# Attention and gated FFN on one core: v kept for two chunks, one limit and one guard for two heads, no empty-row test, the weights' last bits added as integers by GpSimd

## The chip, the cores and the metric

The kernel runs on one core of a Trainium2 chip, as one program. The metric is the device time of one execution in microseconds. The five engines are called as the profile calls them: PE (matmul and transpose; PEld is its weight load), DVE (vector), ACT (scalar, activations), POOL (GpSimd) and SP, which here only issues DMAs. Each engine takes its instructions in the order in which the program lists them, and waits on semaphores for the others.

## The reference, cut to what matters

Eight batches, eight heads, 576 positions, head width 64; the FFN goes from 512 to 1024 and back. The scores are cut at the row's maximum less tau. The softmax sums over what is left, and 1e-9 guards the division.

```python
scores = scale * np.matmul(q, k.transpose(0, 1, 3, 2))
thresh = np.max(scores, axis=-1, keepdims=True) - tau
scores = np.where(scores >= thresh, scores, -1000000000.0)
attn = np.exp(scores - np.max(scores, axis=-1, keepdims=True))
attn = attn / (np.sum(attn, axis=-1, keepdims=True) + 1e-09)
x = np.matmul(attn, v)                      # then heads side by side: (B, S, 512)
...
h = np.maximum(x @ w_in, 0.0)               # (B, S, 1024)
conv_out = sum(conv_w[k] * hp[:, k:k + S, :] for k in range(3))   # hp: h padded by one
out = (h * (1.0 / (1.0 + np.exp(-conv_out)))) @ w_out
```

The weights w_in, conv_w and w_out are 64-bit floats. The kernel gets them as pairs of 32-bit words (low word first) and makes two 32-bit parts, high and low, of each.

## The kernel before, in words

**Tiles.** Heads are taken in pairs, four pairs for a batch. The 576 rows of a pair are five tiles, four of 128 rows and one of 64. The five tiles are cut into two chunks: tiles 0 and 1, and tiles 2 to 4. A *unit* is one tile of one pair (160 in all, 20 for a batch, and units 0 to 7 are batch 0's first chunk). A unit with 128 rows handles the two heads one after the other, the 64-row unit handles both at once.

**A unit** (function `unit`). PE makes the scores of a head into a PSUM buffer `ps_s` (two of them; line 573 in batch 0 and in the 64-row units, line 580 elsewhere). DVE takes the negated maximum into a small tile `few` (588), somebody takes the limit, maximum less tau (594 on DVE or POOL, 592 on ACT), ACT takes the exponential into `em` (597), and DVE masks it against the limit and sums the row (600). Then come three small steps for both heads at once: the guard, sum plus 1e-9 (617), the test for an empty row, 1/576 where the sum is 0 (621), and the reciprocal (624). POOL multiplies `em` by the reciprocal and adds the empty-row term (633, "the norm"). The normalized tile is transposed on PE through `ps_t` (692) and evacuated by ACT into `eT` (687), or, for 28 units, written to DRAM through `parts` and read back transposed by DMA. `attend` multiplies `eT` by v (747, 756).

**v.** `load_v` loads 128x576 words for each pair and chunk, into two buffers in turn, so that each pair's v is loaded twice in a batch.

**The FFN** of a chunk begins when its four pairs are done. `mm1` multiplies by w_in (784), then ACT, DVE and POOL make the gated product in high and low parts (799, 806, 813, 811, 821, 333), and `mm2` multiplies by w_out (842). It is spread between the units of the next chunk.

**The weights** (function `split`, 16 pieces of 128x512 and one of 128x24 for conv_w). A piece arrives as pairs of words in `stage` (one of four buffers) and becomes one 32-bit float `stage_f` in five steps: absolute value of the upper word (ACT, 377), clamp (POOL, 380), shift and mask (DVE, 383), sign and top bit (DVE, 386), and last the top three bits of the lower word put in with an OR (DVE, 389). A copy in reduced precision is the high part (ACT, 400), and the rest is the low part, by PE and ACT for 12 pieces (405, 406, 409) and by POOL for four (333).

**What sets the order.** A planner (`Plan.run`) writes the order of each engine's instructions before the program is built: a list of operations with an engine, an assumed duration, what they read and write, how many buffers a tag has, and a due rank. It goes through assumed time and gives each engine the most urgent operation that is ready. For some operations another engine may step in (limit, guard, norm). The chip then follows these queues in that order, whatever the real durations are. Any edit of an operation or its assumed cost therefore writes all five queues anew.

## Time and profile before

| what | value |
|---|---|
| median of 3 runs | 911.69 us (911.31 to 913.77) |
| span of the profiled execution, first to last instruction | 910.8 us |
| PE busy | 874.6 us, 96% |
| DVE busy | 751.2 us, 82% |
| ACT busy | 673.8 us, 74% |
| POOL busy | 603.5 us, 66% |
| HBM read, written | 58.88 MB, 25.95 MB |

The profile gives the span of the profiled execution; what lies around it is the difference to the time of a run, 0.9 us to the median. Busy shares are means over the whole span. The first 150 us differ from the rest: there batch 0's attention runs beside the preparation of the weights, and the FFN has only begun. The table of slices at the top of the page shows it, and the tables by stretch below are read for that reason.

### The profile page before, as it was taken

How to read it: one execution, taken by the hardware profiler on the slowest of the kernel's cores; microseconds unless marked ns; L12 is line 12 of the kernel's file. 1: busy time of each engine (PE TensorE's matmuls, PEld its weight loads, DVE VectorE, ACT ScalarE, POOL GpSimd, SP SyncE). 2: the span in 40 equal slices, each digit the busy share in tenths (PEclk: the TensorE clock that was granted, in tenths of full speed). 3: DMA queues.
4: the chain of work that ended last, by engine and by line, in shares of the span. 5: the costliest groups of instructions: out<-in, count | busy, mean ns of one | idle time of the engine just before them, and what ended most of it. 6: DMA issues, size and time to landing. Idle time of an engine off the chain costs nothing.

```text
span 910.8 us, 19147 instructions
## 1 busy us (share of the span) xinstructions
PE 874.6 (96%) x6056; PEld 708.6 (78%) x6056; DVE 751.2 (82%) x1871; ACT 673.8 (74%) x1459; POOL 603.5 (66%) x1027
## 2 busy tenths in 40 slices
PE   5978799999999999999999999999999999999998
PEld 3545577878878788888788797887888878887896
DVE  5988999988988689987889789996988779997542
ACT  4878687878777777777768687877867778776642
POOL 2656778875767677685767767776776758675322
PEclk9989899999999999999999999999999999999999
DMA  6555257667764667647665377557667276654000
GB/s 213 155 162 170 57 143 197 149 178 181 198 175 113 163 175 198 158 116 202 169 157 157 117 201 191 140 118 202 173 176 179 89 187 159 181 137 112 13 24 35
DMA packets 148260, 137.02 MB, mean 150 GB/s; under 512 B 85312, under 2 KB 116288, under 8 KB 148160
## 3 DMA queue, kind: packets, MB, share of 16 engines
q1 hardware_dynamic: 147296, 133.90, 55.3%
q10 hardware_dynamic: 864, 1.90, 0.6%
q8 instruction: 49, 0.80, 0.4%
q14 instruction: 51, 0.42, 0.2%
HBM read 58.88 MB, written 25.95 MB: 93 GB/s over the span
## 4 chain that ended last, share of the span: by engine, by line
PE 73%; ACT 8%; DVE 6%; POOL 5%; DMA 4%; issue 3%; SPq 2%; ACTq 0%; POOLq 0%; DVEq 0%
PE po L842 20%; PE ph L784 16%; PE pa L756 12%; PE ps_s L580 11%; PE ps_t L692 9%; PE ps_s L573 3%; ACT em L597 2%; POOL em L633 2%; DVE em L600 2%; ACT eT L687 2%; PE pa L747 2%; DVE few L588 2%; DMA q<-in_qd_dram 1%; SPq L513 1%; DMA q<-q 1%
## 5 line engine op out<-in xcount | busy, mean ns | idle before, releaser
L633 POOL TENSOR_SCALAR em<-em,few 128x576 f32<-128x576 f32 x287 | 262.8, 924 | 29.9 <-DVE few L624 22.1
L600 DVE SCALAR_TENSOR_TENSOR em<-ps_s,few,em 128x576 f32<-128x576 f32 x288 | 230.5, 812 | 25.4 <-ACT em L597 17.1
L588 DVE TENSOR_REDUCE few<-ps_s 128x1 f32<-128x576 f32 x288 | 211.5, 748 | 39.3 <-PE ps_s L573 22.0
L597 ACT ACTIVATE em<-ps_s,few 128x576 f32<-128x576 f32 x288 | 210.5, 741 | 35.8 <-DVE few L588 31.5
L784 PE MATMUL ph<-x,w1h 128*128 128x322 f32 (+1 forms) x1024 | 233.7, 304 | 0.6 <-ACT hp L799 0.5
L687 ACT ACTIVATE eT<-ps_t 128x512 f32<-128x512 f32 (+2 forms) x360 | 168.0, 487 | 24.5 <-PE ps_t L692 22.4
L784 PEld LDWEIGHTS ph<-x,w1h 128*128 128x128 f32 x1024 | 173.1, 189 | 4.7 <-issue 3.0
L692 PE MATMUL ps_t<-ident,em 128*128 128x128 f32 x1060 | 157.8, 280 | 6.5 <-POOL em L633 5.1
L580 PE MATMUL ps_s<-ks,q 128*128 128x288 f32 x896 | 156.8, 306 | 5.3 <-DMA q<-q 2.1
L784 PE MATMUL ph<-x,w1l 128*128 128x322 f32 (+1 forms) x512 | 151.3, 295 | 0.0
L692 PEld LDWEIGHTS ps_t<-ident,em 128*128 128x128 f32 x1060 | 126.5, 143 | 31.5 <-POOL em L633 14.9
L580 PEld LDWEIGHTS ps_s<-ks,q 128*128 128x128 f32 x896 | 129.2, 189 | 20.2 <-issue 8.2
L333 POOL TENSOR_TENSOR gl<-t,gh 128x255 fp32r<-128x255 f32 (+9 forms) x192 | 119.6, 637 | 28.5 <-ACT gh L821 27.5
L756 PE MATMUL pa<-eT,v 128*64 128x320 f32 (+1 forms) x1024 | 132.1, 410 | 0.0
L842 PE MATMUL po<-w2h,gh 128*128 128x512 f32 x288 | 117.9, 409 | 0.3 <-ACT hp L799 0.3
L756 PEld LDWEIGHTS pa<-eT,v 128*64 128x64 f32 x1024 | 70.4, 137 | 59.3 <-issue 15.8
L842 PE MATMUL po<-w2l,gh 128*128 128x512 f32 x288 | 113.3, 393 | 0.0
L842 PE MATMUL po<-w2h,gl 128*128 128x512 f32 x288 | 113.1, 393 | 0.1
L806 DVE SCALAR_TENSOR_TENSOR t<-hp,cr 128x321 f32<-128x321 f32 (+1 forms) x128 | 75.6, 594 | 28.0 <-ACT hp L799 28.0
L784 PEld LDWEIGHTS ph<-x,w1l 128*128 128x128 f32 x512 | 96.8, 189 | 0.2
L813 ACT ACTIVATE t<-t,cm 128x321 f32<-128x321 f32 (+1 forms) x128 | 68.0, 535 | 25.2 <-DVE t L806 12.2
L811 DVE SCALAR_TENSOR_TENSOR t<-t,hp 128x321 f32<-128x321 f32 (+1 forms) x128 | 73.1, 573 | 11.4 <-ACT t L813 9.8
(80 smaller groups left out, 1104.1 us busy)
## 6 DMA issues: line engine op xcount, KB each, us to landing
q<-q SPq DMA_DIRECT2D x336, 64.0 KB, 2.1
v<-in_vc_dram SPq DMA_DIRECT2D x64, 288.0 KB, 3.8
rows<-parts SPq DMA_DIRECT2D x28, 576.0 KB, 3.3
k<-in_kp_dram SPq DMA_DIRECT2D x35, 320.0 KB, 3.5
out_dram<-ot SPq DMA_DIRECT2D x36, 256.0 KB, 2.3
xk<-in_kt_dram SPq DMA_DIRECT2D x28, 288.0 KB, 3.4
ks<-xk SPq DMA_DIRECT2D x56, 144.0 KB, 3.3
xq<-in_qt_dram SPq DMA_DIRECT2D x56, 128.0 KB, 2.9
```

The costliest lines, as they stand in the source:

```text
L333: engines[e].tensor_tensor(dst, x, y, op=ALU.subtract)
L580: nc.tensor.matmul(ps[:, c, :CH], lhsT=q[:, h, o:o + n], rhs=k[:, h, c * CH:(c + 1) * CH], start=(i == 0), stop=(i == 1))
L588: nc.vector.tensor_reduce(few[:rows, nm], ps[:rows, :, :CH], op=ALU.max, axis=mybir.AxisListType.XY, negate=True)
L597: nc.scalar.activation(view(), ps[:rows, :, :CH], AF.Exp, bias=few[:rows, nm])
L600: nc.vector.scalar_tensor_tensor(view(), ps[:rows, :, :CH], few[:rows, th], view(), op0=ALU.is_ge, op1=ALU.mult, accum_out=few[:rows, total])
L633: engines[e].tensor_scalar(sl, sl, by, to, op0=ALU.mult, op1=ALU.add)
L687: "act", act(w, True), lambda dst=dst, src=src: nc.scalar.activation(dst(), src(pt), AF.Copy),
L692: nc.tensor.transpose(out=pt[:, at:at + P], in_=em[:, int(b * P):int(b * P) + P], identity=ident[:])
L756: nc.tensor.matmul(pa[j * D:(j + 1) * D, :w], lhsT=vt[:, blk, :], rhs=eT[:, :w // D, blk, :], start=False, stop=(r == 3))
L784: nc.tensor.matmul(ph[:, :an], lhsT=w1[w][:, cb, fs], rhs=xs[cb][:, h, :an], start=(cb == 0 and i == 0), stop=(cb == NCB - 1 and i == 2))
L806: nc.vector.scalar_tensor_tensor(t[:, :kn], hp[:, k:kn + k], cr[:, j, f:f + 1], y, op0=ALU.mult, op1=ALU.add)
L842: nc.tensor.matmul(po[:], lhsT=x[:, f, at:at + P], rhs=w[:, f, :], start=(f == 0 and i == 0), stop=(f == NFB - 1 and i == 2))
```

## The change: what it does

- `load_v`: the second chunk of batches 1 to 7 takes the v tile that the first chunk loaded. The tag has four buffers in place of two, and 36 loads are left of 64. `parts` has one buffer in place of two, which makes room.
- `unit`: one limit for both heads, a subtraction of two tensors (`ntau` with two columns, less the negated maxima). It reads both heads' maxima, so the first mask now comes after the second maximum.
- The guard is a sum of two tensors, the sums and a constant `least` of 576 x 2^-80. The empty-row test is gone; the norm adds 2^-80 to each weight and multiplies by the reciprocal, which gives 1/576 in an empty row. ACT can no longer take the norm.
- `split`: ACT takes the top 16 bits of the lower word, times 2^-13, as an integer (0 to 8) into the lower word's place (`rounded`), and POOL adds it to `stage_f` as a 32-bit integer (`f4`), where DVE had the OR.
- The planner's assumed DMA times are changed (`put`, `cross`).

```diff
-        op(queue, issue, fn, ring=rows * (n * 0.225 + 4) * 0.0737, **kw)
+        op(queue, issue, fn, ring=rows * n * 0.0149, **kw)
...
+        def rounded():
+            tops = flat().bitcast(U16).rearrange("p (f four) -> p f four", four=4)
+            nc.scalar.activation(words(I32)[0], tops[:, :, 1], AF.Copy, scale=2.0 ** -13)
+
         def f4():
-            nc.vector.scalar_tensor_tensor(v(U32), words()[0], 29, v(U32), op0=ALU.logical_shift_right, op1=ALU.bitwise_or)
+            nc.gpsimd.tensor_tensor(v(I32), v(I32), words(I32)[0], op=ALU.add)
...
+        op("act", act(n), rounded, w=[lo], ahead=w)
...
-        op("dve", 100 + n * 1.3, f4, w=[a], r=[lo], ahead=w, port=True)
+        op("pool", pool(n), f4, w=[a], r=[lo], ahead=w, port=True)
...
     def load_v(i, b, p):
-        vt = plan.buf(wk, "v", 2, [P, NBLK, D], F32, f"v_{i}")
+        if b and chunks[pairs[i][0]].new[0]:
+            return vts[i - NP]
+        vt = plan.buf(wk, "v", VB, [P, NBLK, D], F32, f"v_{i}")
...
-                    engines[e].tensor_scalar(few[:rows, th], few[:rows, nm], -1.0, ntau[:rows], op0=ALU.mult, op1=ALU.add)
+                    subtract(e, few[:rows, limits], ntau[:rows, :m], few[:rows, tops])
...
-            op("dve", 125, limit, w=[(few, ("th", h))], r=[(few, ("nm", h)), (ntau, 0)], ahead=a, other=[("pool", 260), ("act", 110)])
-            op("dve", 738, mask, w=[(em, h), (few, ("sum", h))], r=[(ps, 0), (few, ("th", h))], ahead=a)
+            late.append(mask)
+            if h == m - 1:
+                op(
+                    "dve", 125, limit, w=[(few, "th")], r=[(few, ("nm", x)) for x in range(m)] + [(ntau, 0), (ntau, 1)], ahead=a,
+                    other=[("pool", 260), ("act", 110)]
+                )
+        for h in range(m):
+            op("dve", 738, late[h], w=[(em, h), (few, ("sum", h))], r=[(pss[h], 0), (few, "th")], ahead=a)
...
-            engines[e].tensor_scalar(few[:rows, inverse], few[:rows, sums], 1e-9, 1.0, op0=ALU.add, op1=ALU.mult)
-
-
-        def even(e):
-            engines[e].tensor_scalar(few[:rows, shift], few[:rows, sums], 0.0, 1.0 / S, op0=ALU.is_equal, op1=ALU.mult)
-
+            engines[e].tensor_tensor(few[:rows, inverse], few[:rows, sums], least[:rows, :m], op=ALU.add)
...
-                    engines[e].tensor_scalar(sl, sl, by, to, op0=ALU.mult, op1=ALU.add)
+                engines[e].tensor_scalar(sl, sl, LEAST, few[:rows, 6 + h:7 + h], op0=ALU.add, op1=ALU.mult)
...
-        parts = plan.buf(wk, "parts", 2, [P, 2, 2 * S], U16, f"parts_{u}")
+        parts = plan.buf(wk, "parts", 1, [P, 2, 2 * S], U16, f"parts_{u}")
```

The queues are written anew. Three places show how. The first is POOL's queue while the last eight weight pieces are prepared. `stage_f` is a piece, `em` a unit's weights, `few` its small tile. Before:

```order
L594 TENSOR_SCALAR few_781<-few_781,ntau 128x1 x2
L380 TENSOR_SCALAR stage_f<-stage_f 128x512
L617 TENSOR_SCALAR few_781<-few_781 128x2
L633 TENSOR_SCALAR em_790<-em_790,few_781 128x576 x2
L380 TENSOR_SCALAR stage_f<-stage_f 128x512
L594 TENSOR_SCALAR few_849<-few_849,ntau 128x1 x2
L617 TENSOR_SCALAR few_849<-few_849 128x2
```

The same two units and their neighbours in POOL's queue now (line 399 is the integer add, 386 the clamp, 645 the norm):

```order
L399 TENSOR_TENSOR stage_f<-stage_f,stage_522 128x512
L386 TENSOR_SCALAR stage_f<-stage_f 128x512
L399 TENSOR_TENSOR stage_f<-stage_f,stage_568 128x512
L645 TENSOR_SCALAR em_735<-em_735,few_730 128x576 x2
L386 TENSOR_SCALAR stage_f<-stage_f 128x512
L638 TENSOR_TENSOR few_799<-few_799,least 128x2
L399 TENSOR_TENSOR stage_f<-stage_f,stage_649 128x512
L386 TENSOR_SCALAR stage_f<-stage_f 128x512
L645 TENSOR_SCALAR em_829<-em_829,few_799 128x576 x2
```

Where a unit's small steps stood between clamps and norms, integer adds stand now, two of them ahead of one norm.

The second place is DVE's queue at unit 80, in the middle of the program, before (588 is the maximum, 594 the limit, 600 the mask, 806 a tap of the FFN):

```order
L588 TENSOR_REDUCE few_5674<-ps_s_0_5662 128x1
L588 TENSOR_REDUCE few_5674<-ps_s_1_5669 128x1
L594 TENSOR_SCALAR few_5674<-few_5674,ntau 128x1
L600 SCALAR_TENSOR_TENSOR em_5686,few_5674<-ps_s_0_5662,few_5674,em_5686 128x576
L806 SCALAR_TENSOR_TENSOR t_0_5716<-hp_0_5290,cr 128x255
L600 SCALAR_TENSOR_TENSOR em_5686,few_5674<-ps_s_1_5669,few_5674,em_5686 128x576
```

and now (603, 339 and 615 are the maximum, the limit of both heads and the mask):

```order
L603 TENSOR_REDUCE few_5511<-ps_s_0_5497 128x1
L603 TENSOR_REDUCE few_5511<-ps_s_1_5505 128x1
L339 TENSOR_TENSOR few_5511<-ntau,few_5511 128x2
L615 SCALAR_TENSOR_TENSOR em_5525,few_5511<-ps_s_0_5497,few_5511,em_5525 128x576
L615 SCALAR_TENSOR_TENSOR em_5525,few_5511<-ps_s_1_5505,few_5511,em_5525 128x576
```

The second maximum already stood ahead of the first mask; the tap between the masks has moved behind them.

The third is PE. It has 3878 rows in both, the same matmuls. Ahead of the first score of unit 20, where batch 1 begins, there are 225 rows before and 246 now: 12 more matmuls by w_out (128x512) and 9 more by w_in (128x322) are put ahead of it. Ahead of the first score of unit 60 there are 1106 rows in both.

More of the change, by code (lines that the diff above doesn't have):

```diff
@@ L312, in tile_tau_attention_gated_ffn @@
     op("act", 450, lambda: nc.scalar.dma_start(tau_sb[:], tau.broadcast_to([P, 1])), w=[(tau_sb, 0)], ahead=205.0, late=2500)
-    ntau = const("ntau", [P, 1], F32)
-    op("dve", 70, lambda: nc.vector.tensor_scalar(ntau[:], tau_sb[:], -1.0, None, op0=ALU.mult), w=[(ntau, 0)], r=[(tau_sb, 0)], ahead=6.0)
+    ntau = const("ntau", [P, 2], F32)
+    least = const("least", [P, 2], F32)
+    op("pool", 100, lambda: nc.gpsimd.memset(least[:], LEAST * S), w=[(least, 0)], ahead=200.0)
+    for i in range(2):
+        op("dve", 70, lambda i=i: nc.vector.tensor_scalar(ntau[:, i:i + 1], tau_sb[:], -1.0, None, op0=ALU.mult), w=[(ntau, i)], r=[(tau_sb, 0)], ahead=6.0)
     warm = const("warm", [P, 1], F32)
@@ L558, in unit @@
         em = plan.buf(wk, "em", EMS, [P, 2 * S], F32, f"em_{u}")
-        few = plan.buf(sm, "few", 4, [P, 10], F32, f"few_{u}")
+        few = plan.buf(sm, "few", 4, [P, 8], F32, f"few_{u}")
         a = AHEAD["s" if 2 * n > P else "s4"]
-        tiny = [("pool", 200)]
+        tiny, late, pss = [("pool", 200)], [], []
+        tops, limits = slice(0, m), slice(2, 2 + m)
         for h, js in enumerate(heads):
             ps = plan.buf(ps_s, "ps_s", 2, [P, 2, 512], F32, f"ps_s_{u}_{h}")
+            pss.append(ps)
             nm, th, total = (slice(at + h, at + h + 1) for at in (0, 2, 4))
@@ L588, in top, with limit @@
                 nc.vector.tensor_reduce(few[:rows, nm], ps[:rows, :, :CH], op=ALU.max, axis=mybir.AxisListType.XY, negate=True)
-            def limit(e, nm=nm, th=th):
+            def limit(e):
                 if e == "act":
-                    nc.scalar.activation(few[:rows, th], few[:rows, nm], AF.Identity, scale=-1.0, bias=ntau[:rows])
+                    nc.scalar.activation(few[:rows, limits], few[:rows, tops], AF.Identity, scale=-1.0, bias=ntau[:rows, :1])
                 else:
-                    engines[e].tensor_scalar(few[:rows, th], few[:rows, nm], -1.0, ntau[:rows], op0=ALU.mult, op1=ALU.add)
+                    subtract(e, few[:rows, limits], ntau[:rows, :m], few[:rows, tops])
             def exp(ps=ps, nm=nm, view=view):
@@ L628, in norm @@
                 sl = em[:rows, h * S:(h + 1) * S]
-                by, to = few[:rows, 6 + h:7 + h], few[:rows, 8 + h:9 + h]
-                if e == "act":
-                    nc.scalar.activation(sl, sl, AF.Identity, scale=by, bias=to)
-                else:
-                    engines[e].tensor_scalar(sl, sl, by, to, op0=ALU.mult, op1=ALU.add)
-            choice = {"pool": 807, "dve": 400, "act": 625}
+                engines[e].tensor_scalar(sl, sl, LEAST, few[:rows, 6 + h:7 + h], op0=ALU.add, op1=ALU.mult)
+            choice = {"pool": 807, "dve": 400}
             turns = NORM[u >= NEAR]
@@ L638, in unit @@
             op(
-                home, choice[home], norm, w=[(em, h)], r=[(few, "inverse"), (few, "shift")], ahead=a, port=True,
+                home, choice[home], norm, w=[(em, h)], r=[(few, "inverse")], ahead=a, port=True,
                 other=[(e, ns) for e, ns in choice.items() if e != home]
@@ L664, in cross @@
         put(
-            864, lambda: nc.sync.dma_start(rows[:].rearrange("(q two) k -> q two k", two=2), parts[:]),
+            812, lambda: nc.sync.dma_start(rows[:].rearrange("(q two) k -> q two k", two=2), parts[:]),
             w=[(rows, 0)], r=[(parts, 0), (parts, 1)], ahead=a, late=-500
@@ L670, in turn @@
                 nc.sync.dma_start_transpose(eT[:].bitcast(U16)[:, off // D + j], rows[j * P:(j + 1) * P, :])
-            op("sp", 1560, turn, w=[(eT, (off, j))], r=[(rows, 0)], ahead=a, late=100, ring=1785)
+            op("sp", 1560, turn, w=[(eT, (off, j))], r=[(rows, 0)], ahead=a, late=100, ring=1840)
     def transposes(u, ems, tiles, eT):
```

8 lines of the change are left out of this document (5 added, 3 removed).

## The prediction

> **What bounds the kernel now.** I read the page's totals first, then busy time by stretch, with borders where the program changes: 123.57 us is the first score matmul of batch 1 (unit 20), 142 us the point from which the chain of waits consists of PE's own work, 850 us the end of the attention.
>
> ```profile
> span 910.8 us, 19147 instructions
> PE 874.6 (96%) x6056; PEld 708.6 (78%) x6056; DVE 751.2 (82%) x1871; ACT 673.8 (74%) x1459; POOL 603.5 (66%) x1027
> ...
> core 0: us, PE busy (x) PEld busy (x) DVE busy (x) ACT busy (x) POOL busy (x), PEclk, DMA share, GB/s
> 0.00:123.57 123.57, 100.00 (x589) 60.30 (x589) 103.02 (x247) 90.28 (x185) 72.14 (x119) 0.94 0.48 148
> 123.57:142.00 18.43, 17.00 (x102) 12.70 (x101) 16.64 (x41) 15.88 (x34) 15.35 (x21) 1.00 0.71 204
> 142.00:850.00 708.00, 700.62 (x5027) 586.58 (x5027) 605.61 (x1536) 541.43 (x1175) 499.48 (x850) 1.00 0.62 160
> 850.00:910.80 60.80, 57.01 (x343) 49.07 (x341) 25.95 (x50) 26.20 (x67) 16.56 (x37) 1.00 0.06 23
> ```
>
> From 142 to 850 us PE is busy for 700.62 of 708 us at full clock. The change takes no matmul away, so that stretch can give at most 7.4 us and the tail at most 3.8. The opening is different: PE idles for 123.57 - 100.00 = 23.6 us there, and DVE is the fullest of the other engines (103.02 us, against 90.28 on ACT and 72.14 on POOL). PE's waits there show why it matters:
>
> ```profile
> 52.14 1.33 PE L573 MATMUL ps_s<-k,q 64*128 64x288 f32 x4 [4.63 <-DVE em L600]
> ...
> 103.75 0.72 PE L573 MATMUL ps_s<-k,q 64*64 64x288 f32 x8 [2.00 <-DVE em L600]
> 107.40 1.24 PE L573 MATMUL ps_s<-k,q 64*64 64x288 f32 x8 [2.93 <-issue]
> ...
> 50.00:55.00 5.00, 2.86 (x7) 1.37 (x7) 5.00 (x13) 2.83 (x5) 2.74 (x4) 0.61 0.29 77
> 55.00:60.00 5.00, 5.00 (x21) 3.12 (x19) 2.98 (x8) 4.07 (x8) 1.67 (x4) 0.71 0.46 157
> 105.00:110.00 5.00, 2.60 (x13) 1.01 (x14) 4.91 (x15) 4.11 (x8) 4.28 (x7) 0.57 0.44 117
> 110.00:115.00 5.00, 4.99 (x29) 3.81 (x29) 4.40 (x12) 4.26 (x11) 4.35 (x8) 0.75 0.48 120
> ```
>
> The longest waits are for a mask on DVE, and DVE is full there (5.00 of 5 us, 4.91 of 5). After each the granted clock falls: 5 x (0.39 + 0.29) = 3.4 us of PE time lost once, 5 x (0.43 + 0.25) = 3.4 us again. So the gain or loss is decided in the first 124 us, by the fullest queue.
>
> **The change part by part.** The rows for that opening, 0 to 123.57 us (columns: engine, operation, tiles, count, busy us and mean ns, idle before):
>
> ```profile
> L389 DVE SCALAR_TENSOR_TENSOR stage_f<-stage,stage_f 128x512 uint32<-128x512 uint32 x16 | 13.8, 864 | 0.0
> L594 DVE TENSOR_SCALAR few<-few,ntau 128x1 f32<-128x1 f32 x14 | 2.6, 204 | 0.1
> L621 DVE TENSOR_SCALAR few<-few 128x2 f32<-128x2 f32 (+1 forms) x14 | 2.2, 158 | 0.0
> L617 DVE TENSOR_SCALAR few<-few 128x2 f32<-128x2 f32 (+1 forms) x3 | 0.5, 155 | 0.0
> L806 DVE SCALAR_TENSOR_TENSOR t<-hp,cr 128x255 f32<-128x255 f32 x6 | 4.3, 713 | 0.0
> ...
> L377 ACT ACTIVATE stage_f<-stage 128x512 f32<-128x512 f32 x16 | 10.9, 687 | 3.5 <-POOL w2l L333 3.0 <-DMA stage<-in_w_in_dram 0.5
> L592 ACT ACTIVATE few<-few,ntau 128x1 f32<-128x1 f32 x6 | 1.7, 286 | 0.0
> L631 ACT ACTIVATE em<-em,few 128x576 f32<-128x576 f32 x1 | 0.9, 867 | 0.0
> L524 ACT ACTIVATE xk<-xk 128x576 f32<-128x576 f32 x1 | 0.7, 683 | 0.9 <-DMA xk<-in_kt_dram 0.9
> ...
> L633 POOL TENSOR_SCALAR em<-em,few 128x576 f32<-128x576 f32 x33 | 33.1, 1011 | 4.4 <-DVE few L624 3.2 <-DVE few L594 1.1
> L380 POOL TENSOR_SCALAR stage_f<-stage_f 128x512 f32<-128x512 f32 x16 | 10.5, 658 | 8.0 <-ACT stage_f L377 7.6
> L594 POOL TENSOR_SCALAR few<-few,ntau 128x1 f32<-128x1 f32 x16 | 6.2, 388 | 16.1 <-DVE few L588 14.8 <-DVE few L624 0.8 <-POOL stage_f L380 0.2
> L617 POOL TENSOR_SCALAR few<-few 128x2 f32<-128x2 f32 (+1 forms) x16 | 5.8, 364 | 16.7 <-DVE em L600 16.4 <-DVE few L624 0.2
> L333 POOL TENSOR_TENSOR w2l<-stage_f,w2h 128x512 fp32r<-128x512 f32 x4 | 5.7, 1433 | 3.2 <-ACT w2h L400 3.2
> L333 POOL TENSOR_TENSOR q<-xq,q 128x256 fp32r<-128x256 f32 x2 | 1.6, 822 | 0.0
> L621 POOL TENSOR_SCALAR few<-few 128x2 f32<-128x2 f32 (+1 forms) x5 | 1.1, 227 | 0.6 <-DVE stage_c_f L386 0.4
> ```
>
> *DVE.* The 16 ORs go: -13.8 us. The tests and old guards go: -2.7. The 14 single limits (-2.6) become 14 double ones; such an operation is not in the trace, and its nearest row is the single limit (0.204 us, +2.9; at the 0.155 us of a small step it would be +2.2). By the new order 11 guards stand ahead of unit 20 on DVE, at 0.155 us +1.7 (at 0.204 +2.2), and one tap more (about 0.7). Sum -13.8, so DVE has 103.0 - 13.8 = 89.2 us.
>
> *ACT.* 16 roundings come. None is in the trace; the nearest row (377) has the same shape and reads the same pairs of words, 0.687 us: +11.0 (the longest ACT row above, 0.867 us, gives +13.9; the four limits' 0.286 us, +4.6, is the lower bound). Four limits go (-1.1), the one norm on ACT goes (-0.9), one scaling of k comes earlier (+0.7). Sum +9.7: 100.0 us. ACT takes DVE's place as the fullest.
>
> *POOL.* 16 integer adds come. The nearest row is the two-tensor subtraction of the same shape, 1.433 us: +22.9 (lower bound the one-tensor clamp, 0.658 us, +10.5; upper bound twice the subtraction, +45.9). I take the middle row, because both read two tensors of this size. Of the small steps 13.1 us go (6.2 + 5.8 + 1.1), and 10 guards and 4 limits come (3.6 + 1.6 at 0.364 and 0.388 us). With a norm and a q subtraction that now stand ahead of the border (1.8): 72.1 + 22.9 - 13.1 + 5.2 + 1.8 = 88.9 us.
>
> *The opening's length.* Before, its fullest queue held 103.02 us in 123.57 us, 83.4%. At the same filling ACT's 100.0 us take 119.9 us: -3.6. The lower bound is DVE's whole saving, -13.8; the upper bound is no gain, or the loss of the third rival.
>
> *PE's share.* By the new order 12 matmuls by w_out and 9 by w_in stand ahead of unit 20 in addition, and at unit 60 both orders have the same 1106 rows ahead. Start to start these take 0.23 and 0.15 us:
>
> ```profile
> 130.12 0.40 PE L842 MATMUL po<-w2l,gh 128*128 128x512 f32 x1
> 130.35 0.31 PE L784 MATMUL ph<-x,w1h 128*128 128x322 f32 x1
> 130.50 0.31 PE L784 MATMUL ph<-x,w1l 128*128 128x322 f32 x1
> ```
>
> 12 x 0.23 + 9 x 0.15 = 4.1 us of matmuls move from the stretch where PE is full into one where it idled for 23.6 us: -4.1 if they fit into idle time, 0 if they stand behind a wait.
>
> *Work that lies beside other work: 0.* After 142 us DVE, ACT and POOL hold at most 605.61 of 708 us, and PE covers them; the small steps saved there shorten nothing. The first mask now waits for the second maximum, but in the order before the second maximum already stood ahead of it at unit 80; without that cover it would cost one maximum for a unit where PE waits for the score buffer, and PE's wait for masks is small in the row below. The 28 v loads fewer free SP's queue, where these stood for 31.4 us, but PE waited for DMA only 2.1 us at its largest consumer. One `parts` buffer is free again after 3.3 us, and 28 such units in 708 us come 25 us apart.
>
> ```profile
> L580 PE MATMUL ps_s<-ks,q 128*128 128x288 f32 x896 | 156.8, 306 | 5.3 <-DMA q<-q 2.1 <-DVE em L600 1.1 <-DVE few L594 1.0
> ...
> SPq L549 <- PE pa L756: 31.4, 10, 12.3
> ...
> rows<-parts SPq DMA_DIRECT2D x28, 576.0 KB, 3.3
> ```
>
> **Sum.** Against the profiled execution: 910.8 - 3.6 - 4.1 = 903.1 us of span. The median of the runs, 911.69 us, is 0.9 us above that span; with the same 0.9 I predict **904.0 us**.
>
> **Rivals.** *DVE's whole saving arrives.* Both marked PE waits end early and with them the slow clock: 4.63 + 2.00 + 2.93 us of waiting and twice 3.4 us of half clock, 16.4 us, 895.3 us. For it: both waits name DVE, and the queue loses 13.8 us ahead of them. Against it: ACT grows by 9.7 us in the same stretch, and conv_w's chain of small steps still stands in DVE's queue ahead of unit 8's masks. The Trainium skill ("TensorE: Matmul & The Clock Gate", "The HAM clock gate") states that about 3.4 us of idleness halve PE's clock until some 3.4 us of work have passed. The trace agrees behind the wait of 4.63 us. By that rule a wait cut below 3.4 us would save its own 3.4 us of slow clock too, which is this rival's second half.
>
> *No gain.* The weights' preparation, which has one engine change more for each piece, keeps the opening at its length, and the 4.1 us of matmuls stand behind it: 911.7 us. For it: POOL's clamp already waits for ACT. Against it: every engine's sum is below DVE's 103 us.
>
> *POOL becomes the bound while the last eight pieces are prepared, slower.* Between 60 and 105 us POOL is busy for 30.89 of 45 us:
>
> ```profile
> 60.00:105.00 45.00, 38.89 (x260) 24.53 (x258) 40.03 (x81) 34.04 (x71) 30.89 (x43) 1.00 0.38 120
> ...
> POOL stage_f L380 <- ACT stage_f L377: 7.6, 7, 2.2
> ...
> L333 POOL TENSOR_TENSOR w2l<-stage_f,w2h x4: 1265/1356/1754, 91.2 to 105.0; 128x512 fp32r<-128x512 f32 x4
> ```
>
> Eight adds come (11.5 us), and by the order seven limits and five other small steps go there (about 4.5). Each add waits for two other engines, as a clamp does (7.6 us in 7 waits, 1.1 each, 8.7 us for eight), and holds the norms behind it, for which PE's transposes wait. If an add takes 1.75 us (the longest w2l subtraction, 1754 ns, is 0.32 above the mean; 2.6 us for eight), the stretch needs 30.9 + 11.5 - 4.5 + 8.7 + 2.6 = 49.2 us in place of 45. Then nothing of the rest arrives and the time is 911.7 + 4.2 = 915.9 us. It decides from the point where POOL's queue in this stretch exceeds 45 us. The Trainium skill ("GPSIMD Engine Reference", "Engine selection") advises against two-input elementwise work on GpSimd, about half as fast as VectorE. The rows here say 1433 against 864 ns, a ratio of 1.66; by its factor an add would take 1.7 us, an estimate from that page, and this rival would come closer.
>
> **How the numbers follow.** Forecast 0.50 (own range 899 to 909), whole saving 0.14, no gain 0.18, POOL 0.18. From 896 to 915 us: below lies the larger half of the whole saving (about 0.08), above the larger half of the POOL case (about 0.10). A measurement of this kernel can tell about 0.3%, 2.7 us, from no change: faster is below 909.0 us. The forecast (nearly all) and the first rival give 0.63, no gain 0.20 with the forecast's edge, and POOL 0.17.
>
> **What would show it.** In the changed profile: DVE below 92 us ahead of batch 1's first score, ACT near 100, POOL near 89; that score at about 120 us; the add at 1.3 to 1.75 us and the rounding near 0.69; PE as full as now after 142 us. The forecast is wrong if the score comes at 123 us or later, if an add takes over 1.8 us, or if PE idles more than 8 us between 142 and 850 us.

## The result, and the profile after

The changed kernel takes 928.21 us (median of 4 runs, 926.53 to 929.77), the kernel before beside it 912.51 us. The ratio is 1.016, with a 95% interval of 1.0134 to 1.0185: slower by 15.7 us, where 904.0 was forecast and 915 was the upper end of the range.

The page's totals and, from the table by stretch with borders that answer to those of before (121.30 us is batch 1's first score matmul now), the four stretches of the changed kernel; the columns are busy us and counts of PE, PEld, DVE, ACT and POOL, then PE's clock, the DMA share and GB/s:

```profile
span 928.0 us, 18745 instructions
PE 883.2 (95%) x6056; PEld 709.4 (76%) x6056; DVE 776.8 (84%) x1727; ACT 677.3 (73%) x1450; POOL 560.0 (60%) x911
```

```profile
0.00:121.30 121.30, 100.35 (x609) 60.67 (x610) 102.94 (x227) 97.81 (x200) 79.33 (x113) 1.00 0.49 157
121.30:142.00 20.70, 17.25 (x91) 13.01 (x92) 18.64 (x40) 15.94 (x32) 15.32 (x22) 0.84 0.67 178
142.00:850.00 708.00, 691.20 (x4898) 572.63 (x4899) 618.20 (x1384) 527.34 (x1135) 444.13 (x733) 1.00 0.55 146
850.00:928.00 78.00, 74.42 (x461) 63.05 (x459) 37.04 (x79) 36.23 (x86) 21.20 (x44) 0.99 0.10 31
```

Three things are to be seen. Batch 1's first score comes 2.3 us earlier than before (121.30 against 123.57), with more matmuls ahead of it. Between 142 and 850 us PE idles for 16.8 us in place of 7.4 and gets through 129 matmuls fewer (4898 against 5027); they stand in the last stretch, which is 17.2 us longer. And DVE is busy for 25.6 us more in all (776.8 against 751.2) though it has 144 instructions fewer. By the first maximum of each unit the loss grows over the whole program: unit 20 comes 2.6 us earlier than before, unit 60 3.2 us later, unit 100 5.2, unit 140 11.5 and unit 159 17.4.

An engine with fewer instructions and more busy time has instructions that got longer. The groups of DVE in the changed kernel's whole span show which (line, engine, operation, tiles, form, count, busy us and mean ns, idle before):

```profile
L339 DVE TENSOR_TENSOR few<-ntau,few 128x2 f32<-128x2 f32 (+1 forms) x125 | 44.2, 355 | 2.4
```

Line by line, with the shortest, median and longest ns, first the limit of the changed kernel and then the limit of the kernel before:

```profile
L339 DVE TENSOR_TENSOR few<-ntau,few x125: 142/162/1398, 11.6 to 861.1; 128x2 f32<-128x2 f32 x106, 128x1 f32<-128x1 f32 x19
```

```profile
L594 DVE TENSOR_SCALAR few<-few,ntau x170: 195/207/216, 8.6 to 842.6; 128x1 f32<-128x1 f32 x170
```

At its median the new limit is shorter than the old one (162 against 207 ns). But 48 of the 125 take more than 250 ns, and 6 take more than 1 us. The time line around one of them, in the changed kernel (start us, duration us):

```profile
315.75 1.44 POOL L339 TENSOR_TENSOR xk<-xk,ks 128x576 fp32r<-128x576 f32 x1 [1.44 <-ACT ks L536]
315.81 1.40 DVE L339 TENSOR_TENSOR few<-ntau,few 128x2 f32<-128x2 f32 x1
317.31 0.82 DVE L615 SCALAR_TENSOR_TENSOR em<-ps_s,few,em 128x576 f32<-128x576 f32 x1
```

The limit has two columns to subtract. It starts 0.06 us behind a GpSimd instruction and ends 0.02 us behind that one's end, and the mask waits behind it in DVE's queue. So it is with all 48: a GpSimd instruction was running when they started, and they end 10 ns (median) after one ends. Of the 170 limits of the kernel before, 133 started while GpSimd ran, and none took more than 216 ns.

Not every limit beside GpSimd waits. Of the changed kernel's 125, 68 started with more than 250 ns of a GpSimd instruction still to go, and 48 of these waited. The other 20 all stood beside a norm that had 686 ns or more to go, where the shortest norm takes 741 ns in all and the limits that did wait for a norm found at most 640 ns left. So it seems that the one whose work begins first goes first; no run tests that.

PE's waits between 142 and 850 us in the changed kernel (line waited, for what, us in total, times, longest):

```profile
PE ps_s L595 <- DMA q<-q: 6.1, 5, 2.1
PE ps_s L595 <- DVE em L615: 4.0, 9, 1.1
...
PE ps_t L704 <- POOL em L645: 1.5, 3, 0.8
PE ps_t L704 <- DVE x L778: 1.4, 2, 0.8
```

Before, the first two were 2.1 us in one wait and 1.1 us in two. PE waits longer for masks, and longer for the DMAs that bring q; what delays the latter was not followed up.

### The profile page after: what moved, and what is told of

Its sections match the earlier page's. It is cut to its first block, busy times and chain, and to the rows that moved or that the text cites. A ratio compares the mean times of both kernels' runs of the same rounds, so it can differ in the third digit from the quotient of the medians.

```text
span 928.0 us, 18745 instructions
## 1 busy us (share of the span) xinstructions
PE 883.2 (95%) x6056; PEld 709.4 (76%) x6056; DVE 776.8 (84%) x1727; ACT 677.3 (73%) x1450; POOL 560.0 (60%) x911
## 4 chain that ended last, share of the span: by engine, by line
PE 67%; DVE 13%; DMA 7%; ACT 6%; issue 3%; SPq 2%; POOL 2%; ACTq 0%; DVEq 0%; POOLq 0%
PE po L854 19%; PE ph L796 14%; PE ps_s L595 11%; PE pa L768 9%; PE ps_t L704 9%; DVE few L603 4%; DVE em L615 4%; DMA q<-q 3%; PE ps_s L588 3%; ACT em L612 2%; PE pa L759 2%; DVE t L818 2%; DMA q<-in_qd_dram 1%; ACT eT L699 1%; SPq L682 1%
## 5 line engine op out<-in xcount | busy, mean ns | idle before, releaser
L645 POOL TENSOR_SCALAR em<-em,few 128x576 f32<-128x576 f32 x287 | 234.9, 829 | 133.7 <-DVE few L641 125.2
L612 ACT ACTIVATE em<-ps_s,few 128x576 f32<-128x576 f32 x288 | 208.0, 742 | 52.2 <-DVE few L603 47.8
L615 DVE SCALAR_TENSOR_TENSOR em<-ps_s,few,em 128x576 f32<-128x576 f32 x288 | 225.5, 813 | 15.9 <-ACT em L612 6.2
L595 PE MATMUL ps_s<-ks,q 128*128 128x288 f32 x896 | 160.0, 310 | 13.8 <-DMA q<-q 6.1
L339 POOL TENSOR_TENSOR gl<-t,gh 128x255 fp32r<-128x255 f32 (+9 forms) x192 | 123.1, 652 | 32.4 <-ACT gh L833 31.3
L818 DVE SCALAR_TENSOR_TENSOR t<-hp,cr 128x321 f32<-128x321 f32 (+1 forms) x128 | 83.2, 654 | 20.5 <-ACT hp L811 20.4
L818 DVE SCALAR_TENSOR_TENSOR t<-hp,cr,t 128x321 f32<-128x321 f32 (+1 forms) x128 | 92.8, 728 | 0.6
```

The lines of the kernel that those rows point to most:

```text
L339: engines[e].tensor_tensor(dst, x, y, op=ALU.subtract)
L595: nc.tensor.matmul(ps[:, c, :CH], lhsT=q[:, h, o:o + n], rhs=k[:, h, c * CH:(c + 1) * CH], start=(i == 0), stop=(i == 1))
L612: nc.scalar.activation(view(), ps[:rows, :, :CH], AF.Exp, bias=few[:rows, nm])
L615: nc.vector.scalar_tensor_tensor(view(), ps[:rows, :, :CH], few[:rows, th], view(), op0=ALU.is_ge, op1=ALU.mult, accum_out=few[:rows, total])
L645: engines[e].tensor_scalar(sl, sl, LEAST, few[:rows, 6 + h:7 + h], op0=ALU.add, op1=ALU.mult)
L818: nc.vector.scalar_tensor_tensor(t[:, :kn], hp[:, k:kn + k], cr[:, j, f:f + 1], y, op0=ALU.mult, op1=ALU.add)
```

## The experiments

Ratios are to the kernel before, on the same chip in the same series, with their 95% intervals; the kernel before took 913.0 to 913.7 us in four of the five series and 915.6 in the fourth.

### The form of the limit: r1, r2, r13

In the changed kernel's own order, DVE's limit as one operation for each head with one tensor (r1), or the subtraction issued twice (r2, the removed line here a second time for DVE):

```diff
-                    subtract(e, few[:rows, limits], ntau[:rows, :m], few[:rows, tops])
+                    if e == "dve":
+                        for x in range(m):
+                            nc.vector.tensor_scalar(few[:rows, 2 + x:3 + x], few[:rows, x:x + 1], -1.0, ntau[:rows, :1], op0=ALU.mult, op1=ALU.add)
+                    else:
+                        subtract(e, few[:rows, limits], ntau[:rows, :m], few[:rows, tops])
```

> The changed kernel with all five queues in the same order, but where DVE takes the limit of both heads it does so with two one-tensor operations of one column each (as the kernel before did for one head) in place of one subtraction of two tensors. Nothing of the computation is left out. Theory A (the two-tensor limit waits on DVE for POOL's running instruction to end; 48 of 125 limits took over 250 ns, 44.3 us in all): the single ones take about 0.21 us each whatever POOL does, DVE's instructions behind them start earlier, and some 5 to 12 us of the 16 come back: 916 to 923 us. Theory B (the planner's new DMA prices put the q copies too late) and theory C (the integer adds on POOL): no change, 926 to 930 us, or a little more, because DVE has 106 instructions more.

> The changed kernel in the same order, with every limit on DVE issued twice (same operands, same result). Theory A: DVE's limits cost 44.3 us once; the second of two finds POOL's instruction ended more often than not, so 0.16 to 0.35 us for each of 125, 20 to 44 us more on DVE; where the limit is on the path that PE waits for, the time rises by 6 to 20 us, to 934 to 948 us. If the limit lies beside other work (theories B and C), the time rises by less than 4 us, to 932 us at most.

r1: 919.52 us, ratio 1.0065 (1.0045 to 1.0085), 0.95% or 8.7 us below the changed kernel. r2: 954.98 us, 1.0454 (1.0436 to 1.0472), 27 us above it. The groups of r1 and of r2:

```profile
L611 DVE TENSOR_SCALAR few<-few,ntau 128x1 f32<-128x1 f32 x231 | 38.3, 204 | 0.3
```

```profile
L339 DVE TENSOR_TENSOR few<-ntau,few 128x2 f32<-128x2 f32 (+1 forms) x250 | 94.7, 380 | 6.7
```

And the stretch from 142 to 850 us of r1, then of r2:

```profile
142.00:850.00 708.00, 696.12 (x4985) 580.99 (x4984) 617.52 (x1501) 534.34 (x1151) 447.24 (x739) 1.00 0.56 148
```

```profile
142.00:850.00 708.00, 678.46 (x4784) 557.42 (x4782) 634.13 (x1452) 513.51 (x1106) 428.87 (x712) 1.00 0.56 146
```

231 operations of 204 ns do the work of 125 of 355 ns, none is longer than 215 ns, and PE idles for 11.9 us in place of 16.8. The second of two limits in a row stalls even more often than the first: 46 of the 125 first ones and 64 of the second ones take over 250 ns, each of them started while GpSimd ran. r2's time went beyond its expectation (934 to 948): 50.5 us of added DVE work cost 27, though DVE has 74 us of slack in that stretch.

The same form in the other kernel tells whether it needs the joint limit:

```diff
-                    engines[e].tensor_scalar(few[:rows, th], few[:rows, nm], -1.0, ntau[:rows], op0=ALU.mult, op1=ALU.add)
+                    if e == "dve":
+                        nc.vector.tensor_tensor(few[:rows, th], ntau[:rows], few[:rows, nm], op=ALU.subtract)
+                    else:
+                        engines[e].tensor_scalar(few[:rows, th], few[:rows, nm], -1.0, ntau[:rows], op0=ALU.mult, op1=ALU.add)
```

> The kernel before in its own order; the 170 limits that DVE does become two-tensor subtractions of one column (minus tau less the negated maximum), nothing else changes. Theory A (an operation of DVE with two tensors in SBUF waits for a running GpSimd instruction, whatever its size and place): mean of these limits 0.33 to 0.42 us in place of 0.208, DVE busy 20 to 35 us more, the time 922 to 940 us. Rival (the stall belongs to the joint limit, which comes behind the second maximum): mean 0.15 to 0.21, time 911 to 915.

921.42 us, ratio 1.0058 (1.0036 to 1.008), and its group:

```profile
L595 DVE TENSOR_TENSOR few<-ntau,few 128x1 f32<-128x1 f32 x170 | 50.8, 310 | 0.9
```

62 of the 170 now take over 250 ns, all with GpSimd running. The mean, 310 ns, lies between the two expectations, nearer the theory's 330 to 420. The time misses the theory's 922 to 940 by little, and DVE's busy time, 767.9 against 751.2 us, rises by 16.7 us where at least 20 were expected. The mechanism holds for one column and without the joint limit, its price is smaller there. The stall belongs to the form.

### DMA prices and the weights: r3, r4, r6, r11

r3 puts the planner's old DMA prices into the changed kernel:

```diff
-        op(queue, issue, fn, ring=rows * n * 0.0149, **kw)
+        op(queue, issue, fn, ring=rows * (n * 0.225 + 4) * 0.0737, **kw)
...
```

> The changed kernel with the planner's assumed DMA times of the kernel before; all queues are written anew. Theory B (PE waits 6.1 us for the copies of q where it waited 2.1 before, because the new prices let the planner put them later): back to 914 to 921 us. Theories A and C: 925 to 931 us, a change of order by itself being worth some 2 us either way.

928.25 us, 1.0165 (1.014 to 1.0189): the time doesn't move, though the order is another one (2347 of PE's 6056 weight loads differ, place by place, from the changed kernel's). So not every new order costs time.

r4 gives the OR back to DVE in the changed kernel; r6 puts rounding and integer add, and nothing else, into the kernel before:

```diff
-            nc.gpsimd.tensor_tensor(v(I32), v(I32), words(I32)[0], op=ALU.add)
+            nc.vector.scalar_tensor_tensor(v(U32), words()[0], 29, v(U32), op0=ALU.logical_shift_right, op1=ALU.bitwise_or)
...
-        op("act", act(n), rounded, w=[lo], ahead=w)
...
```

> The changed kernel with the weights' last bits put in by DVE's OR as before, without the rounding on ACT and the integer add on POOL; all queues are written anew. Theory C (the adds cost the time): back to 914 to 920 us. Theory A or B: the opening gets longer again, since batch 1's first maximum came at 122.2 us with 4 us more of PE work done than in the kernel before, where it came at 124.8: 930 to 937 us.

> The kernel before with the part on the weights alone: the OR of the last bits leaves DVE, ACT rounds them to integers and GpSimd adds them; limits, guards, masks, v and parts are as before. In the changed kernel, putting this part back cost 10.6 us, so by the theory that this part gains and the two-source operations lose, this kernel takes 900 to 906 us and is faster than before, with unit 20's first maximum some 3 to 6 us earlier. By the rival, that GpSimd's longer work of the first 120 us (16 adds at 1.28 us) costs what DVE gains once DVE has its old limits, it takes 910 to 914.

r4: 938.78 us, 1.0283 (1.0257 to 1.031), 10.6 us above the changed kernel and above both of its ranges. r6: 921.82 us, 1.0087 (1.0066 to 1.0109), 8 us above the kernel before and above both of its ranges. One edit with both signs can't be read as the price of this part: both kernels are planned anew. r11 therefore holds the order. The planner sees the kernel before, and only the operations issued differ; PE's and SP's rows are the same as before, one for one.

```diff
             nc.scalar.activation(v(), words(F32)[1], AF.Abs)
+            tops = flat().bitcast(U16).rearrange("p (f four) -> p f four", four=4)
+            nc.scalar.activation(words(I32)[0], tops[:, :, 1], AF.Copy, scale=2.0 ** -13)
...
-            nc.vector.scalar_tensor_tensor(v(U32), words()[0], 29, v(U32), op0=ALU.logical_shift_right, op1=ALU.bitwise_or)
+            nc.gpsimd.tensor_tensor(v(I32), v(I32), words(I32)[0], op=ALU.add)
```

> The part on the weights in the order of the kernel before: the planner sees the kernel before; where it issues DVE's OR, GpSimd's integer add is issued, and ACT's rounding right behind ACT's absolute value. The order of TensorE and of the DMA queue is unchanged. Theory E: the part gains once the order is held, 901 to 908 us. Rival F (GpSimd's 16 adds of 1.28 us in the opening cost what DVE gains): 912 to 920, like the replanned kernel with this part (921.8).

919.58 us, 1.0063 (1.0041 to 1.0086): slower again, and here the place is sharp. Unit 12 comes 1.3 us late, unit 16 6.1 us late, and from there to unit 159 the lag grows by only 2.1 us more, to 8.2. The stretch between is that in which the last weight pieces are prepared. DVE's waits there (78 to 107 us), in the kernel before the one for the clamp, then the two longest in r11:

```profile
DVE stage_f L383 <- POOL stage_f L380: 0.6, 1, 0.6
```

```profile
DVE stage_f L386 <- POOL stage_f L383: 7.8, 5, 3.3
DVE em L603 <- ACT em L600: 4.2, 2, 2.7
```

Up to 125 us DVE is busy for 14 us less than in the kernel before (90.12 against 104.45) and has got through 36 instructions fewer. It waits for GpSimd's clamp, which stands among the 16 adds (21.2 us, 1323 ns each) in GpSimd's queue, and for ACT's exponential. GpSimd isn't full there (35.86 of 45 us between 60 and 105 us): in the order of before, the adds make it late by their place in the queue, not by their sum.

### Guard, place of the limit, v: r5, r8, r7

r5 is r1 with the guard, too, as one-column operations with one tensor. r8 has that guard, and a limit for each head planned apart, with the mask behind its own limit (the two planned lines that the change's diff removes, put back). r7 is the kernel before with v kept and one `parts` buffer (the lines of `load_v` and of `parts` in the change's diff). The edit of r5 beside r1's:

```diff
-            engines[e].tensor_tensor(few[:rows, inverse], few[:rows, sums], least[:rows, :m], op=ALU.add)
+            if e == "dve":
+                for x in range(m):
+                    nc.vector.tensor_scalar(few[:rows, 6 + x:7 + x], few[:rows, 4 + x:5 + x], LEAST * S, 1.0, op0=ALU.add, op1=ALU.mult)
+            else:
+                engines[e].tensor_tensor(few[:rows, inverse], few[:rows, sums], least[:rows, :m], op=ALU.add)
```

> The changed kernel in the changed kernel's order, with both of DVE's small two-tensor operations, the limit and the guard, issued as one-column operations with one tensor each (add 2^-80 times S, times 1). It tells apart where the 6.5 us lie that remained between the kernel with one-column limits (919.5 us) and the kernel before (912 to 913). Theory D1 (the guard stalls behind GpSimd as the limit did): the 78 guards take 20.8 us in the changed kernel, and 13 of them are long; as two one-column operations at about 0.15 us they take no stall, DVE's work per unit falls or stays, and the time comes to 914 to 917 us. Theory D2 (the two heads' limit in one: the first mask waits for the second maximum, whatever the form of the operation): 918 to 921, as with the one-column limit alone. No limit or guard should take more than 0.25 us.

> The changed kernel with a limit for each head, planned by itself as before (each mask waits for its own head's maximum alone), and the guard as one-column operations with one tensor; weights, v, parts and the missing test of empty rows stay as changed. Theory D2 (the joint limit loses by its place): 903 to 909 us, below the kernel with one-column limit and guard in the joint order by 8 us or more. Theory D1 (only the stalls behind GpSimd lose): within 3 us of that kernel. If the loss that remains comes from v and parts or the order of the rest, both stay above 912.

> The kernel before with v kept for both chunks (36 loads in place of 64) and one buffer for parts; all else as before. If v and parts are worth nothing, as predicted, it takes 910 to 914 us. If the one parts buffer holds up the packing of the transposes that go through the DMA queue (a theory for the steady loss of 0.06 us per unit that remained with one-column limits), it takes 915 to 920. If the loads that are gone help the queue, 906 to 910.

r5: 918.78 us, 1.0047 (1.0025 to 1.0069), within the uncertainty of r1's. Its guards take 135 to 156 ns, where 13 of the 78 two-tensor guards were long; DVE's busy time falls by 5.6 us (766.29 to 760.66) and the time hardly; that is theory D2's number. r8: 922.06 us, 1.0082 (1.0061 to 1.0104): giving each mask its own limit brings nothing, where theory D2 asked for 8 us or more. So neither theory is borne out. As r8 is planned anew, a gain that is smaller than the scatter of plans, shown below, isn't excluded. r7: 919.44 us, 1.0059 (1.004 to 1.0078): slower by 6 us, though it takes 28 loads away. The time is that of the theory of the held-up `parts` buffer, but the trace speaks against it: the copies into `parts` wait 0.8 us in all there, for the norm.

### The order by itself: r9, r10, r14, r15, r16

Every kernel so far that was planned anew and lacks the two-tensor limit (r1, r5, r6, r7, r8) came out 4 to 8 us above the kernel before, by whatever it differed. So r9 and r10 change one number that the planner reads, by 7 ns, and no instruction:

```diff
-            op("dve", 738, mask, w=[(em, h), (few, ("sum", h))], r=[(ps, 0), (few, ("th", h))], ahead=a)
+            op("dve", 745, mask, w=[(em, h), (few, ("sum", h))], r=[(ps, 0), (few, ("th", h))], ahead=a)
```

r10 does the same with the maximum (668 to 675).

> The kernel before, every operation as it was, with one number of the planner changed: a mask is planned at 745 ns in place of 738. No work is added or removed; only the order that the planner writes differs. Theory E (what remained of the loss is the order: the kernel before happens to have a good one, and any change of a price draws another, at some 4 to 9 us more, as in the three kernels that differ from it by the weights, by v, or by the single limits): 915 to 922 us. Rival F (the order is worth little; each part had a cost of its own): 911 to 914.

> The same with another number: a maximum is planned at 675 ns in place of 668, the mask at 738 as before. Theory E: 915 to 922 us, and not the same loss at the same units as with the mask's price. Rival F: 911 to 914.

r9: 918.66 us, 1.0066 (1.004 to 1.0091). r10: 917.59 us, 1.0043 (1.0023 to 1.0063). Nothing but the order differs, and 4 to 6 us are lost. The stretch from 142 to 850 us in r9, then in r10:

```profile
142.00:850.00 708.00, 698.68 (x4994) 580.78 (x4993) 612.23 (x1532) 539.23 (x1169) 496.66 (x851) 1.00 0.61 160
```

```profile
142.00:850.00 708.00, 698.96 (x4990) 579.69 (x4991) 611.71 (x1517) 542.67 (x1174) 500.27 (x864) 1.00 0.61 161
```

PE idles for 9.3 and 9.0 us there, where the kernel before has 7.4. The same prices in the changed kernel without its stalls (r14 and r15 are r5 with 745 and with 675, r16 is r8 with 745):

> The changed kernel with limit and guard as one-column operations (918.8 us), the mask planned at 745 ns in place of 738: another order of the same instructions. If the 6 us over the kernel before are the order, and the rest of the change gains, 907 to 916; if the rest of the change is worth nothing, 916 to 922, like the kernel before with the same price (918.7).

> The same with the maximum planned at 675 ns in place of 668. Gain of the rest: 907 to 916. No gain: 916 to 922 (the kernel before with this price took 917.6).

> The changed kernel with a limit planned for each head and the guard as one-column operations (922.1 us), the mask planned at 745 ns. Gain of the rest: 907 to 916. No gain: 916 to 924.

r14: 925.64 us, 1.0109 (1.0088 to 1.0129). r15: 920.93 us, 1.0067 (1.0046 to 1.0089). r16: 930.2 us, 1.0158 (1.0139 to 1.0177). r14 and r16 lie above even their "no gain". None falls below the kernel before, none even below r5. Five plans of the changed kernel without two-tensor steps on DVE (r5, r14 and r15 with the joint limit, r8 and r16 with one for each head) span 1.0047 to 1.0158, and two new orders of the kernel before 1.0043 and 1.0066. The rest of the change is no gain that shows above the scatter of the order.

### Only taking away: r12, r17, r18

r12 is r11 without the empty-row test. r17 is the kernel before in its own order without the test, with guard and norm adding 2^-80 and the OR left on DVE; r18 is r17 with one-column guards on DVE (r5's edit). The test's part of the edit:

```diff
-            engines[e].tensor_scalar(few[:rows, shift], few[:rows, sums], 0.0, 1.0 / S, op0=ALU.is_equal, op1=ALU.mult)
+            pass
...
-                if e == "act":
-                    nc.scalar.activation(sl, sl, AF.Identity, scale=by, bias=to)
-                else:
-                    engines[e].tensor_scalar(sl, sl, by, to, op0=ALU.mult, op1=ALU.add)
+                (nc.vector if e == "act" else engines[e]).tensor_scalar(sl, sl, LEAST, by, op0=ALU.add, op1=ALU.mult)
```

> As the run above, in the order of the kernel before, and besides the test for empty rows is not issued (93 operations of DVE, 67 of GpSimd), the guard adds 2^-80 times S, and a row is normalised by adding 2^-80 and multiplying, as in the changed kernel; the guard keeps one tensor for both heads. Theory E: 897 to 906 us, 0 to 5 below the run above, since the tests' 14.9 us of DVE lie mostly beside TensorE. Rival F: 911 to 919.

> The kernel before in its own order, without the test for empty rows (93 operations of DVE of 0.16 us, 67 of GpSimd of 0.23 us): guard and normalisation add 2^-80 as in the changed kernel, the OR of the weights stays on DVE, limits and v as before. Nothing is added and nothing is moved. If work that is taken from DVE in the opening is worth its time there: 909 to 912 us beside a kernel before at 913 (ratio 0.996 to 0.999). If the order is fitted to its own durations, so that any shift loses: ratio 1.002 or more.

> As the run above, and the guards on DVE are one-column operations (2 of about 0.15 us in place of one of 0.29 us on two columns, 17 of whose 69 were long while GpSimd ran). Ratio to the kernel before 0.995 to 0.999 if the two-column guard's stalls cost something, and the same as the run above, within 0.002, if they lie beside TensorE.

r12: 918.51 us, 1.0051 (1.0031 to 1.0071), about 1 us below r11, not resolved. r17: 913.02 us beside 913.67, 0.9988 (0.9974 to 1.0003). r18: 913.11 us, 0.9991 (0.9976 to 1.0006). 160 small operations taken out, in an order that is kept but for one norm that goes from ACT to DVE, change nothing that can be measured. That part of the forecast, steps that lie beside PE's work, holds. No kernel here beats the kernel before.

## Why the prediction was wrong, step by step

**What bounds the kernel: half right.** PE is the bound after 142 us, and the opening did not lose. But "the gain or loss is decided in the first 124 us" is wrong: unit 20 came 2.6 us earlier, and 20 us were lost between there and unit 159. One reading was loose, too: PE's longest single wait in the opening of before is not for a mask, but the 6.4 us for ACT's q at the start; for masks it waits longest in sum (9.0 us in four waits).

**The step that failed: the price of the limit, and with it "Work that lies beside other work: 0".** The double limit was priced at the single one's 0.204 us, or 0.155. In the opening, for which that price was used, it measured 0.242, and over the whole program 0.355, because an operation of DVE on two SBUF tensors can wait for a running GpSimd instruction. Since the limit stands between maximum and mask, the wait holds the mask, the score buffer behind the mask, and PE. In the sum the limits after 142 us counted as 0; the run with the one-tensor form in the same order (r1) gives the form 8.7 us over the whole program. The forecast named the bound for it, PE idle above 8 us between 142 and 850; it was 16.8. The row that warned was in the trace of before, in the guard that the change replaced:

```profile
L617 DVE TENSOR_SCALAR few<-few x69: 139/169/1390, 16.0 to 845.7; 128x2 f32<-128x2 f32 x51, 128x1 f32<-128x1 f32 x18
```

A median of 169 ns with a longest of 1390 is no price for a small step: 17 of these 69 took over 250 ns, each with GpSimd running. I took the 0.155 us of the three that stand in the opening.

**DVE's sum: wrong by its whole size.** 89.2 us were forecast ahead of batch 1's first score, 102.94 measured. The ORs' 13.8 us are gone, and longer rows filled most of the time again. DVE's groups in the changed kernel from 0 to 121.30 us:

```profile
L392 DVE SCALAR_TENSOR_TENSOR stage_f<-stage,stage_f 128x512 uint32<-128x512 uint32 x16 | 13.2, 822 | 0.1
L389 DVE TENSOR_SCALAR stage_f<-stage_f 128x512 uint32<-128x512 uint32 x16 | 9.8, 611 | 0.1
L818 DVE SCALAR_TENSOR_TENSOR t<-hp,cr 128x255 f32<-128x255 f32 x7 | 6.0, 861 | 0.4 <-ACT hp L811 0.4
L818 DVE SCALAR_TENSOR_TENSOR t<-hp,cr,t 128x255 f32<-128x255 f32 x6 | 5.9, 992 | 0.0
L823 DVE SCALAR_TENSOR_TENSOR t<-t,hp 128x255 f32<-128x255 f32 x5 | 4.0, 808 | 0.2 <-ACT t L825 0.2
L339 DVE TENSOR_TENSOR few<-ntau,few 128x2 f32<-128x2 f32 (+1 forms) x14 | 3.4, 242 | 0.2
L638 DVE TENSOR_TENSOR few<-few,least 128x2 f32<-128x2 f32 (+1 forms) x11 | 3.4, 306 | 0.2
```

and those of the kernel before, ahead of its own border, that the prediction didn't show:

```profile
L386 DVE SCALAR_TENSOR_TENSOR stage_f<-stage,stage_f 128x512 uint32<-128x512 uint32 x16 | 12.5, 784 | 0.0
L383 DVE TENSOR_SCALAR stage_f<-stage_f 128x512 uint32<-128x512 uint32 x16 | 7.7, 488 | 1.6 <-POOL hp L794 0.9 <-POOL stage_f L380 0.6
...
L806 DVE SCALAR_TENSOR_TENSOR t<-hp,cr,t 128x255 f32<-128x255 f32 x6 | 3.7, 612 | 0.0
L811 DVE SCALAR_TENSOR_TENSOR t<-t,hp 128x255 f32<-128x255 f32 x5 | 3.0, 592 | 0.6 <-ACT t L813 0.4
```

The same taps take 861 and 992 ns in place of 713 and 612, the shift 611 in place of 488. These groups hold 45.7 us now and 36.5 before, tests and guards counted: 9.2 of the 13.8 us have come back, one tap more among them. With the OR back on DVE and no adds on GpSimd (r4), ahead of 125 us, the taps and the shift are short again:

```profile
L389 DVE TENSOR_SCALAR stage_f<-stage_f 128x512 uint32<-128x512 uint32 x16 | 7.9, 493 | 3.6 <-POOL stage_f L386 3.5
L813 DVE SCALAR_TENSOR_TENSOR t<-hp,cr,t 128x255 f32<-128x255 f32 x6 | 4.4, 735 | 0.0
L813 DVE SCALAR_TENSOR_TENSOR t<-hp,cr 128x255 f32<-128x255 f32 x7 | 4.4, 628 | 0.0
L392 DVE SCALAR_TENSOR_TENSOR stage_f<-stage,stage_f 128x512 uint32<-128x512 uint32 x16 | 13.9, 871 | 0.1
```

The sign step (last row) is not: 871 ns, longer than in the other two. r4 has another order again, so it doesn't tell the adds from the order. r11 does, with the adds in the order of before (up to 130 us, by which it has done the same 16 pieces and 12 taps):

```profile
L389 DVE SCALAR_TENSOR_TENSOR stage_f<-stage,stage_f 128x512 uint32<-128x512 uint32 x16 | 13.3, 829 | 0.0
L386 DVE TENSOR_SCALAR stage_f<-stage_f 128x512 uint32<-128x512 uint32 x16 | 9.8, 615 | 8.0 <-POOL stage_f L383 8.0
L809 DVE SCALAR_TENSOR_TENSOR t<-hp,cr 128x255 f32<-128x255 f32 x6 | 4.5, 758 | 0.0
L809 DVE SCALAR_TENSOR_TENSOR t<-hp,cr,t 128x255 f32<-128x255 f32 x6 | 3.2, 532 | 0.0
```

The shift takes 615 ns there and the sign step 829, 2.9 us more for the 16 pieces than before; the taps don't get longer in sum (7.7 us against 8.0). So the part on the weights lengthens its own other steps on DVE and not the taps. What makes the taps long in the changed kernel, its order or the adds at the place that the order gives them, is open.

**The single prices on ACT and POOL: right.** The rounding took 698 ns (0.687), the add 1331 (1433, inside its range), ACT's queue 97.81 us (100.0), POOL's 79.33 (88.9; eight guards and four limits stood there, and the norms were shorter).

**The opening's length and PE's share: right in size, not by their reason.** -3.6 and -4.1 us were forecast. The score came at 121.30 (forecast "about 120"), with the 4.1 us of matmuls ahead of it. But -3.6 rests on a fullest queue that gets shorter, and it did not, since DVE stayed at 103 us. What did go are the two waits that the prediction marked: behind the first unit, no wait of PE in the changed kernel's opening exceeds 2.1 us, and the granted clock of the opening is 1.00 (0.94 before). By the prediction's own sum the two slow stretches had cost 3.4 us each, 6.8 us together, and 2.3 + 4.1 us were gained; no run separates whether that is why. One slow stretch came back just behind the opening, after a wait for a norm:

```profile
125.77 2.00 PE L704 MATMUL ps_t<-ident,em 128*128 128x128 f32 x8 [2.94 <-POOL em L645]
...
125.00:130.00 5.00, 4.24 (x20) 4.05 (x20) 4.97 (x11) 2.48 (x5) 4.04 (x6) 0.50 0.64 157
130.00:135.00 5.00, 5.00 (x28) 2.52 (x27) 3.58 (x9) 4.54 (x10) 4.37 (x7) 0.83 0.54 161
```

**What is left of the loss: as large as a new order costs, its cause open.** Of the 15.7 us, 8.7 are the limit's form. What the two-tensor guard adds lies within the uncertainty (r1 against r5, 919.52 and 918.78 us). The 4 to 6 us that r5 and r1 still lose are as much as two new orders of the kernel before cost, without any change of an instruction (r9, r10): the kernel before has an order that none of the other plans tried here reaches. That the order is the cause in r5 and r1 too is not shown: they also hold the part on the weights, which costs 6 us in the order of before (r11). The forecast compared the two orders at three places and gave the new order no price of its own. Which rows of the order cost these microseconds is open, and so is whether an order exists in which the changed kernel gains.

**The rivals.** None of the three named this mechanism. "No gain" was nearest for the changed kernel without its stalls. Of "DVE's whole saving arrives" the two waits and their slow clock did go, and the saving on DVE did not come. "POOL becomes the bound", forecast for 60 to 105 us, did not happen in the changed kernel, where POOL is busy for 34.04 of these 45 us. r11 loses 4.8 us at about that place, between units 12 and 16, where 4.2 were worked out; but its POOL, too, is below 45 us there (35.86), so the rival's condition isn't met, and that the sizes agree is luck.

## What to carry to other kernels

Price a small operation by its longest and its count of long ones, not by its median, and ask of each form how many SBUF tensors it reads while GpSimd works: merging two short one-tensor steps into one two-tensor step can cost more than it saves. Work moved to GpSimd can also lengthen what stays on VectorE (in r11 the shift, from 488 to 615 ns). Where a planner writes the order, redraw the old kernel's order with a price off by one per cent before reading a change of less than one per cent, and test a part in the held order.

## What the runs showed of the hardware

- A VectorE operation that reads two SBUF tensors can wait for the running GpSimd instruction, even if it has one column: 62 of 170 with one column in r13 (up to 1.16 us), 110 of 250 with one or two columns in r2 (up to 1.40 us). The long ones end about 10 ns after the GpSimd instruction does.
- With one tensor and one column none waited: none of 170 in the kernel before, of 231 and 144 in r5, of 120 in r18 was longer than 216 ns, though GpSimd ran at the start of 133, 176, 52 and 50 of them. With one tensor and two columns it depends on the operation: in the kernel before 17 of 69 guards and 2 of 93 tests (TENSOR_SCALAR) took over 250 ns, all with two columns and GpSimd running, but none of the changed kernel's 128 two-column reciprocals took more than 168, though 17 of them started with over 250 ns of a GpSimd instruction to go. The one-column guards of r18 and the reciprocals of the changed kernel, line by line:

```profile
L620 DVE TENSOR_SCALAR few<-few x120: 135/148/156, 16.1 to 846.3; 128x1 f32<-128x1 f32 x120
...
L641 DVE RECIPROCAL few<-few x160: 145/156/168, 14.9 to 863.5; 128x2 f32<-128x2 f32 x128, 128x1 f32<-128x1 f32 x32
```

- The Trainium skill states this rule ("SBUF — State Buffer", "Who interferes with whom"): VectorE with two SBUF inputs contends with a GpSimd instruction that reads SBUF, with one input it does so only in a two-port mode, and the loser blocks for the whole instruction. The traces agree for the limits that waited, not for the 20 of 68 in the changed kernel that went ahead beside a norm. That the two-column form of the guard runs in such a mode fits the page "VectorE: DVE Perf Modes" (section "Mode 2×_2P", an even outermost dimension); no run here shows the mode itself. By that rule the change's two merged steps would have been priced with a wait wherever GpSimd is running, which speaks against this change.
- GpSimd's 32-bit integer add of 128x512 takes 1.33 us, its float subtraction of the same shape 1.46 in the same stretch of the changed kernel (5.9 us for four).
- The granted clock of PE also fell at waits shorter than the 4.63 us that the prediction worked with: to 0.50 between 125 and 130 us, at the wait of 2.94 us shown above, and to 0.62 between 784 and 788 us, at a wait of 2.14 us for q's DMA, both in the changed kernel.
